# Batch 1 of a sliding-window attention with a gated feed-forward put into the form of batches 2 and 3

## The chip, the cores and the metric

The kernel runs on one core of one Trainium2 chip. The metric is the device time of one execution in microseconds, the median of three runs. A profiled execution gives the trace that the prediction reads.

## The reference

Attention over 4 batches, 8 heads, 768 tokens and heads of 64, in which a query sees the first four tokens (the sinks) and the 128 tokens that end with itself; then a feed-forward without a nonlinearity, whose two gates are multiplied. Inputs and output are float32.

```python
scores = scale * np.matmul(q, k.transpose(0, 1, 3, 2))
keep = (pos[None, :] < 4) | ((rel >= 0) & (rel < 128))       # rel = query - key
a = softmax(np.where(keep, scores, -1e9))
x = np.matmul(a, v).transpose(0, 2, 1, 3).reshape(B * S, H * D)   # 3072 x 512
out = ((x @ w1) * (x @ w2)) @ w3 @ w_out                     # d_ff = 1024
```

## The kernel before

Everything is computed in bfloat16 with float32 sums. `w3 @ w_out` is folded into one matrix `w3o` at the start: the tasks `t3` transpose w3 by row blocks (`fold_w3`), `fm` multiply (`fold_mm`). Its inputs come as raw float32 through SP's queue, with casts on ACT and DVE, or through POOL's queue, which casts in the transfer. Between the first tasks, while the weights arrive, `keep_busy` issues filler matmuls (`pz`).

Then, for each batch:

- POOL issues the loads of k, q (`kqN`) and v (`vN`), a block of 128 tokens each, 128 KB in the chip's memory format. From batch 2 on, a load first waits until the load four before it has landed (`send_load`, the small copies into `spent`).
- k and q are needed with the head's dimension on the partitions (`kqT`). Batches 0 and 1 turn a block with eight TensorE transposes and one DVE copy of PSUM (task `tpk`, line 260 and 262). Batches 2 and 3 turn it with one DMA transpose on SP's queue (task `td`, line 267).
- Scores (`sc`): matmuls of 64 rows, exp on ACT, a mask on DVE. Values (`av`): matmuls, then a reciprocal and a product on DVE that write `xn`. Batches 0 and 1 work by 256 queries, in `scores` and `values` (or by 128 in `block_scores`), and treat the sinks apart: sink scores `ss` (line 312), their exp `es`, sink values `vs`, and one matmul of 130 columns in each `av` beyond the first 256 tokens. Batches 2 and 3, those in `LATE`, work by the units of `CUTS` (320, 224, 224 tokens: `UNITS`, `SPANS`), in `late_scores` and `late_values`. There a block's own keys are copied behind the four sink keys (`own_keys`, task `ko`, tile `kown`), and its values likewise in `vp` and `vN` (`own_values`, task `vo`), so that the sinks need no matmul of their own.
- x is turned: batch 0 with TensorE and a copy on ACT (`xt`), batches 1 to 3 with DMA transposes (`xd`, line 511).
- Gates (`g`, line 524): for each chunk of tokens and each of 8 column blocks, four matmuls with w1, copied by ACT, and four with w2, multiplied on DVE into `ab`. Chunks: 3 x 256 tokens in batches 0 and 1; 320 and 448 in batches 2 and 3.
- Projection (`p`, line 585): eight matmuls of 512 columns for 128 tokens, a copy and an output DMA on SP's queue.

TensorE's order is written out by hand, task by task, in `TURNS`. The order on ACT, DVE and SP follows from a planner in the kernel (`plan`), which runs while the program is built: it has a duration for each stage and an arrival time for each load (`landings`, `service`), picks what could start first, and `LEAN` shifts single choices. Engines run their instructions in that fixed order, so what waits at the head of a queue holds up what stands behind it. PSUM has four buffers for ordinary tasks (`mm`) and two for scores (`sc`). A change between score matmuls and others in TensorE's order is called a turn.

Buffers are shared by tags: `kqN`, `kqT`, `xT`, `ab` and `kown` alternate between two batches, `vp` lies where `wo_sb` was, and `w3T` uses `kown` and `kqN` of batches whose loads come later.

Of the kernel before, what the change touches and what calls it, by code (L numbers as in the profile page):

```python
# [21 lines left out]
def kernel(  # L22
# [13 lines left out]
    nc = tc.nc  # L36
# [17 lines left out]
    LATE = range(2, B)  # L54
# [6 lines left out]
    CHUNKS = [[(256 * i, 256 * i + 256) for i in range(3)]] * 2 + [[SPANS[0], (SPANS[1][0], S)]] * (B - 2)  # L61
    XPOSE = ((2, 0), (2, 1), (2, 2), (3, 0), (3, 1), (3, 2))
# [17 lines left out]
    vc = const.tile([P, 2, D], FP32, name="vc")  # L80
# [23 lines left out]
    vp = [None] * 2 + [inp.tile([P, 4, H, VS], BF16, tag="wo", bufs=1, name=f"vp_{b}") for b in LATE]  # L104
    kown = [None] * 2 + [inp.tile([P, NP, 5, P], BF16, tag=f"kown{b % 2}", bufs=1, name=f"kown_{b}") for b in LATE]
    ksbd = [inp.tile([P, 648], BF16, name=f"ksbd_{b}") for b in range(2)]
    vs = [inp.tile([P, H, D + 1], BF16, name=f"vs_{b}") for b in range(2)]
    es = [inp.tile([P, 512], BF16, name=f"es_{b}") for b in range(2)]
# [15 lines left out]
    def send_load(b, dst, src):  # L124

        if b in LATE and len(sent) >= AHEAD:
            nc.gpsimd.tensor_copy(spent[:], sent[-AHEAD])  # L127
        nc.gpsimd.dma_start(out=dst, in_=src)  # L128
        sent.append(dst[:, 0, 0:1])

    def load_qkv(b, kb):
        for src, dst in ((k, kN), (q, qN)):
            send_load(b, heads(dst[b][:, kb, :]), rows(src, b, kb * P, (kb + 1) * P))
        for s in VSLOTS[kb] if b in LATE else (kb,):
            t0, t1 = KEYS[s] if b in LATE else (kb * P, (kb + 1) * P)
            send_load(b, vN[b][:, s, :, 0:D], rows(v, b, t0, t1))
# [18 lines left out]

    def load(what, *i):
        if what == "qkv":
            if i[1] == 0:
                nc.gpsimd.memset(vN[i[0]][:, :, :, D:VS], 1.0)
            for kb in range(i[1], i[2]):  # L160
                load_qkv(i[0], kb)
# [70 lines left out]
    for b in range(2):  # L232
        nc.gpsimd.tensor_copy(vs[b][:, :, D], ones_s[:])
    for h in range(H):
        r0 = 32 * (h // 2) + 4 * (h % 2)
        nc.sync.dma_start(out=vc[r0:r0 + 4, :, :], in_=v[0:2, h, 0:4, :].rearrange("b s d -> s b d"))
# [17 lines left out]

    def transposes(b, kb):

        tp = ps_mm.tile([P, 2, NP, P], BF16, tag="mm", name="tp")
        for i, src in enumerate((kN[b], qN[b])):
            for r in range(NP):
                nc.tensor.transpose(tp[:, i, r, :], src[:, kb, r * P:(r + 1) * P], ident)  # L260
        yield
        nc.vector.tensor_copy(kqT[b][:, :, :, kb * P:(kb + 1) * P], tp[:])  # L262
# [89 lines left out]
    def late_values(b, r, u):  # L352
# [28 lines left out]
        if r == 0:  # L381
# [50 lines left out]
    def block_values(b, j, r0):  # L432
# [19 lines left out]
        if i == 0 and r0 == 0:  # L452
# [5 lines left out]
    def block_x_transposes(b, j):  # L458
# [6 lines left out]
        nc.scalar.copy(xT[b][:, :, j * P:(j + 1) * P], xt[:])  # L465
        yield

    def values(b, r, t):
# [20 lines left out]
        if r == 0:  # L489
# [5 lines left out]
    def x_transposes(b, r0, t):  # L495

        xt = ps_mm.tile([P, 2, 2, P], BF16, tag="mm", name="xt")
        for r in range(2):
            for i in range(2):
# [4 lines left out]
        nc.scalar.copy(xT[b][:, r0:r0 + 2, t * 256:(t + 1) * 256],  # L504
                       xt[:].rearrange("p r i m -> p r (i m)"))
        yield

    def x_transposes_dma(b, t, i):

        q0, q1 = QB[UNITS[t][i]] if b in LATE else (t * 256 + i * P, t * 256 + i * P + P)  # L510
# [26 lines left out]
    def fold_w3(i, j0, j1):  # L537
# [5 lines left out]
        if i not in w3T:  # L543
            w3T[i] = (flat(kqN[1], "k i s")[:, i * 1024:i * 1024 + 1024].rearrange("p (k n) -> p k n", n=P)
                      if i in (4, 5) else flat(kown[2 + i % 6 // 2], "r m x")[:, i % 2 * 1024:][:, 0:1024].rearrange("p (k n) -> p k n", n=P))
        nc.vector.tensor_copy(w3T[i][:, j0:j1, :], tp[:])  # L546
# [13 lines left out]
    def fold_mm(i, j0, j1):  # L560
# [13 lines left out]
        if j1 == KFF and i >= 4:  # L574
            nc.scalar.copy(w3o[:, i, :], po)
            yield
        elif j1 == KFF and i % 2:
            nc.scalar.copy(w3o[:, i - 1:i + 1, :], held[i // 2][:])
            yield

    def project(b, m, n0, n1):
# [7 lines left out]
        (nc.vector.tensor_copy if n0 == DM // 2 else nc.scalar.copy)(o_sb, po[:])  # L589
# [18 lines left out]
    def service(what, *i):  # L608
        if what == "qkv":
            late = i[0] in LATE  # L610
            return [(0.95 if i[0] == 0 else 0.87 * n, 0.845 * n if 6 * i[0] + kb < 14 else (2.15 if i[0] == 2 else 1.9) * n, [(x, i[0], s)])
                    for kb in range(i[1], i[2])
                    for x, s, n in [("k", kb, 1.0), ("q", kb, 1.0)]
                    + [("v", s, 1.0) for s in (VSLOTS[kb] if late else (kb,))]]
# [6 lines left out]
    def landings(RAW=2.0, POOL=3.0, DGE=1.3, RAMP=(0.75, 1.0)):  # L621
# [6 lines left out]
        while any(at[n] < len(q) for n, q in queues.items()):  # L628
# [11 lines left out]
            for n in busy:  # L640
# [3 lines left out]
                if left[n][at[n]] <= 0.0:  # L644
                    lag, keys = queues[n][at[n]][2:]
                    for key in keys:
                        arrive[key] = now + lag + min(1.5, max(0.0, 0.25 * (now - 36.0))) + min(3.0, max(0.0, 0.1 * (now - 70.0))) + min(4.5, max(0.0, 0.2 * (now - 112.0)))
# [28 lines left out]
    for i in range(KFF):  # L676
        for h in range(2):
# [3 lines left out]
                 [("pe", 0.057 * (j1 - j0)), ("dve", 0.05 + 0.075 * (j1 - j0))],  # L681
                 [x for a, _ in needs for x in a], [x for _, a in needs for x in a],
                 started=[("t3", i, 0)] if i >= SPLIT and h else [folded(i - SPLIT)] if i >= SPLIT else [], ring="mm")
        for h, (j0, j1) in enumerate(FM[i]):
# [4 lines left out]
                 [("pe", 0.216 * (j1 - j0))] + ([("act", 0.6 if i >= 4 else 1.04)] if last and (i % 2 or i >= 4) else []),  # L689
# [6 lines left out]
            if last and (i % 2 or i >= 4):  # L696
                tasks["fm", i, h]["frees"] = ("fm", i if i >= 4 else i - 1, 0)
    unit = []
    last_av = []
    late = []  # L700
    for b in range(B):
        for t in range(NT):
            kbs = (2 * t, 2 * t + 1)
            qk = []
            war = [("av", b - 2, NP - 1, NT - 1)] if b >= 2 else []
            for kb in kbs:
                if (b, t) in XPOSE:
                    qk.append(("td", b, kb))
                    task(qk[-1], 1, transposes_dma(b, kb), [("sp", 2.6), ("dma", 1.2)], war, [("k", b, kb), ("q", b, kb)])
                else:  # L710
                    qk.append(("tpk", b, kb))
                    task(qk[-1], 1, transposes(b, kb), [("pe", 0.45), ("dve", 0.65)],
                         war, [("k", b, kb), ("q", b, kb)], "mm")
            if b in LATE:
                def turned(what, kbs):
                    if (b, 0) in XPOSE:
                        return [("td", b, kb) for kb in kbs]
                    return [("tpk", b, kb) for kb in kbs]
# [9 lines left out]
            else:  # L728
# [3 lines left out]
                elif t == 1:  # L732
                    more = [(n, b, kb) for n in (("td",) if (b, 2) in XPOSE else ("tpk",)) for kb in (4, 5)]
# [320 lines left out]
```

## Time and profile before

| what | us |
|---|---|
| median of three runs | 195.2 (194.99 to 195.25) |
| profiled execution, device time | 194.77 |
| its span in the profile | 193.1 |
| TensorE busy in the span | 186.6 |
| DVE busy | 120.9 |
| ACT busy | 101.9 |
| POOL busy | 88.4 |

The page's parts are: engines' busy time, the span in 40 slices, DMA queues, the chain of work that ended last, and groups of instructions. PE is TensorE, and L followed by a number is a line of the kernel. In a group's row the figures after the bar are busy time, the mean duration of one in nanoseconds, and the idle time of the engine just before them with what ended it. In the chain and in a timeline a row has its start and its length. The granted TensorE clock is full in all slices.

### The profile page before, as it was taken

How to read it: one execution, taken by the hardware profiler on the slowest of the kernel's cores; microseconds unless marked ns; L12 is line 12 of the kernel's file. 1: busy time of each engine (PE TensorE's matmuls, PEld its weight loads, DVE VectorE, ACT ScalarE, POOL GpSimd, SP SyncE). 2: the span in 40 equal slices, each digit the busy share in tenths (PEclk: the TensorE clock that was granted, in tenths of full speed). 3: DMA queues.
4: the chain of work that ended last, by engine and by line, in shares of the span. 5: the costliest groups of instructions: out<-in, count | busy, mean ns of one | idle time of the engine just before them, and what ended most of it. 6: DMA issues, size and time to landing. Idle time of an engine off the chain costs nothing.

```text
span 193.1 us, 4791 instructions
## 1 busy us (share of the span) xinstructions
PE 186.6 (97%) x1879; PEld 123.6 (64%) x1879; DVE 120.9 (63%) x293; ACT 101.9 (53%) x172; POOL 88.4 (46%) x149
## 2 busy tenths in 40 slices
PE   7999989999999999999999999999999999999993
PEld 2454556898768777786987767655555666555442
DVE  4753777846898979668777677474666865223300
ACT  3142279653984867357438664366356562243222
POOL 4399787699997866645764875400000000000000
PEclk9999999999999999999999999999999999999999
DMA  5999999999999999999999999994540033320034
GB/s 222 415 367 171 170 162 197 195 160 154 154 177 170 122 161 132 197 235 141 179 142 142 225 212 143 224 165 137 125 57 0 3 88 94 96 93 0 0 122 149
DMA packets 109718, 29.42 MB, mean 152 GB/s; under 512 B 100352, under 2 KB 105600, under 8 KB 109696
## 3 DMA queue, kind: packets, MB, share of 16 engines
q0 software_dynamic: 81600, 12.59, 97.7%
q1 hardware_dynamic: 27952, 16.47, 36.6%
q8 instruction: 14, 0.23, 0.5%
q10 hardware_dynamic: 144, 0.07, 0.1%
q14 instruction: 8, 0.07, 0.1%
HBM read 29.90 MB, written 6.29 MB: 187 GB/s over the span
## 4 chain that ended last, share of the span: by engine, by line
PE 85%; DMA 8%; POOL 4%; SPq 1%; issue 0%; ACT 0%
PE pg L524 44%; PE po L585 22%; DMA w_sb<-in_moe_w_dram 4%; DMA ab<-in_moe_w_out_dram 3%; PE av L376 3%; PE sc L341 3%; PE av L484 3%; PE tp L260 2%; PE sc L392 2%; POOL kqN L128 2%; PE pw L571 2%; PE av L447 1%; PE sc L414 1%; POOL vN L128 1%; SPq L192 1%; PE xt L463 1%
## 5 line engine op out<-in xcount | busy, mean ns | idle before, releaser
L524 PE MATMUL pg<-xT,w_sb 128*128 128x256 bf16 (+2 forms) x640 | 92.7, 294 | 0.0
L524 PEld LDWEIGHTS <-w_sb 128*128 128x128 bf16 x640 | 59.4, 98 | 22.5 <-issue 0.6
L528 DVE TENSOR_TENSOR ab<-a_sb,pg 128x256 bf16<-128x256 f32 (+2 forms) x80 | 37.4, 472 | 35.9 <-PE pg L524 29.6
L531 ACT COPY a_sb<-pg 128x256 f32<-128x256 f32 (+2 forms) x80 | 33.2, 418 | 36.7 <-PE pg L524 35.7
L585 PE MATMUL po<-w3o,ab 128*128 128x512 bf16 (+2 forms) x208 | 44.4, 363 | 0.0
L585 PEld LDWEIGHTS <-ab 128*128 128x128 bf16 x208 | 19.3, 98 | 18.8 <-issue 0.2
L589 ACT COPY w_sb<-po 128x512 f32<-128x512 f32 (+2 forms) x25 | 14.1, 565 | 24.3 <-PE po L585 24.2
L128 POOL DMA_DIRECT2D vN<-in_v_dram x26 | 23.4, 898 | 3.4 <-issue 1.6
L344 ACT ACTIVATE ex<-sc 128x928 bf16<-128x928 f32 (+1 forms) x24 | 22.6, 973 | 4.3 <-PE sc L341 3.6
L128 POOL DMA_DIRECT2D kqN<-in_k_dram x24 | 21.7, 905 | 2.7 <-issue 1.3
L128 POOL DMA_DIRECT2D kqN<-in_q_dram x24 | 21.7, 906 | 2.5 <-issue 1.3
L397 ACT ACTIVATE ex<-sc 128x1024 bf16<-128x1024 f32 (+1 forms) x16 | 15.2, 973 | 3.8 <-PE sc L392 3.4
L348 DVE TENSOR_TENSOR am<-ex,maskt 128x928 bf16<-128x928 bf16 (+1 forms) x24 | 15.2, 652 | 3.1 <-ACT ex L344 3.1
L383 DVE TENSOR_TENSOR xn<-av,rec 112x256 bf16<-112x256 f32 (+1 forms) x24 | 11.2, 468 | 0.8
L127 POOL CAST spent<-kqN 128x1 f32<-128x1 bf16 x24 | 5.5, 228 | 10.7 <-DMA kqN<-in_q_dram 6.2
L402 DVE TENSOR_TENSOR am<-ex,maskt 128x1024 bf16<-128x1024 bf16 (+1 forms) x16 | 10.1, 650 | 0.1
L376 PEld LDWEIGHTS <-am 128*128 128x128 bf16 x208 | 8.9, 98 | 1.7
L262 DVE COPY kqT<-tp 128x1024 bf16<-128x1024 bf16 x12 | 8.3, 688 | 1.6 <-PE tp L260 1.5
L376 PE MATMUL av<-vN,am 128*128 128x65 bf16 x144 | 9.1, 193 | 0.0
L418 ACT ACTIVATE ex<-sc 128x1024 bf16<-128x1024 f32 x7 | 7.2, 1029 | 3.2 <-PE sc L414 3.2
L571 PE MATMUL ph<-wo_sb,kown 128*128 128x512 bf16 x32 | 8.4, 379 | 0.3 <-DVE kown L546 0.3
L602 PE MATMUL pz<-ksbd 128*128 128x512 bf16 x19 | 6.8, 509 | 1.3 <-DVE ksbd L201 1.3
(83 smaller groups left out, 192.6 us busy)
## 6 DMA issues: line engine op xcount, KB each, us to landing
out_dram<-w_sb SPq DMA_DIRECT2D x20, 256.0 KB
vN<-in_v_dram POOLq DMA_DIRECT2D x26, 128.0 KB, 6.0
kqN<-in_k_dram POOLq DMA_DIRECT2D x24, 128.0 KB, 6.0
kqN<-in_q_dram POOLq DMA_DIRECT2D x24, 128.0 KB, 6.6
w_sb<-in_moe_w_dram POOLq DMA_DIRECT2D x9, 256.0 KB, 8.3
ab<-in_moe_w_dram SPq DMA_DIRECT2D x4, 512.0 KB
ab<-in_moe_w_out_dram SPq DMA_DIRECT2D x2, 512.0 KB
kqN<-in_moe_w_out_dram SPq DMA_DIRECT2D x2, 512.0 KB
```

Of the source, the lines that this page charges most:

```text
L128: nc.gpsimd.dma_start(out=dst, in_=src)
L344: nc.scalar.activation(ex[:, :, 0:n], sc[:, :, 0:n], ACTF.Exp, scale=scale)
L348: nc.vector.tensor_mul(am[:, :, 0:n], ex[:, :, 0:n], maskt[:, mv:mv + 1, 0:n].to_broadcast([P, 2, n]))
L376: nc.tensor.matmul(o, lhs, rhs, start=(x == 0), stop=(x == len(todo) - 1), skip_group_check=True)
L383: nc.vector.tensor_mul(xns[b, u][0:m, 0:n, r, :, :], av[0:m, :, :, 0:D], rec[0:m, 0:n].to_broadcast([m, n, 2, D]))
L397: nc.scalar.activation(ex[:, :, c0:], sc[:, :, c0:], ACTF.Exp, scale=scale)
L524: nc.tensor.matmul(pg[:], w_sb[:, kk, dt * P:(dt + 1) * P], xT[b][:, kk, tk], start=(kk == 0), stop=(kk == NP - 1))
L528: nc.vector.tensor_mul(ab[b][:, dt, tk], gate_a.pop((b, c, dt))[:], pg[:])
L531: nc.scalar.copy(a_sb[:], pg[:])
L571: nc.tensor.matmul(po, w3T[i][:, j, :], wo_sb[:, j, :], start=(j == 0), stop=(j == KFF - 1))
L585: nc.tensor.matmul(po[:], ab[b][:, kk, m * P:(m + 1) * P], w3o[:, kk, n0:n1], start=(kk == 0), stop=(kk == KFF - 1))
L589: (nc.vector.tensor_copy if n0 == DM // 2 else nc.scalar.copy)(o_sb, po[:])
```

## The change

Batch 1 joins `LATE`: its scores, values and copies of own keys and values take the form of batches 2 and 3, and its sink tiles (`vs`, `es`, half of `vc`) and sink tasks go. Its gates are cut in three chunks, 320, 224 and 224 tokens. Of its k and q, blocks 0 to 2 are still turned by TensorE and blocks 3 to 5 now by DMA transposes. Of its x, the first 320 tokens are turned by TensorE (`late_x_transposes`, new) and the rest, as before, by DMA. Its loads are issued with v one block behind k and q, seven of v instead of six, and still without the wait on the fourth load before. `OTHER` names copies that change from ACT to DVE or back. `TURNS` is written anew for the whole kernel, `LEAN` has a shift for nearly every choice, and the planner's arrival times change. `w3T` now uses `kown` of batches 2 and 1. `PAIRED` is empty, so its branches do nothing.

```diff
-    LATE = range(2, B)
+    LATE = range(1, B)
...
-    CHUNKS = [[(256 * i, 256 * i + 256) for i in range(3)]] * 2 + [[SPANS[0], (SPANS[1][0], S)]] * (B - 2)
-    XPOSE = ((2, 0), (2, 1), (2, 2), (3, 0), (3, 1), (3, 2))
+    CHUNKS = [[(256 * i, 256 * i + 256) for i in range(3)], SPANS] + [[SPANS[0], (SPANS[1][0], S)]] * (B - 2)
+    TURNED = ((1, 3), (1, 4), (1, 5)) + tuple((b, kb) for b in (2, 3) for kb in range(NB))
+    PAIRED = ()
...
-    X_XPOSE = ((1, 0), (1, 1), (1, 2), (2, 0), (2, 1), (2, 2), (3, 0), (3, 1), (3, 2))
+    X_TURNED = ((1, 1), (1, 2)) + tuple((b, u) for b in (2, 3) for u in range(NT))
...
+    OTHER = {("fm", 1, 3), ("fm", 7, 3), ("p", 2, 2), ("p", 2, 3), ("p", 2, 5), ("p", 3, 1), ("p", 3, 2), ("p", 3, 4),
+             ("t3", 0, 1), ("t3", 1, 1), ("t3", 2, 1), ("t3", 3, 1), ("t3", 5, 0), ("t3", 6, 1), ("t3", 7, 1), ("tpk",
+             0, 1), ("tpk", 1, 1), ("xt", 0, 0, 0), ("xt", 0, 2, 0), ("xt", 0, 2, 2), ("xt", 1, 0, 0)}
...
-        if b in LATE and len(sent) >= AHEAD:
+        if b >= 2 and len(sent) >= AHEAD:
...
+    def pieces(b, kb0, kb1):
+
+        lag = 1 if b == 1 else 0
+        return [x for n in range(kb0, kb1 + lag)
+                for x in ([("kq", n)] if n < kb1 else []) + ([("v", n - lag)] if n - lag >= kb0 else [])]
...
+    def copier(name, act):
+
+        return nc.scalar.copy if act != (name in OTHER) else nc.vector.tensor_copy
...
+    def late_x_transposes(b, u, i):
+
+        q0, q1 = QB[UNITS[u][i]]
+        m = q1 - q0
+        xt = ps_mm.tile([P, NP, m], BF16, tag="mm", name="xt")
+        for r in range(NP):
+            nc.tensor.transpose(xt[:, r, :], xns[b, u][0:m, i, r, :, :].rearrange("p e d -> p (e d)"), ident[0:m, 0:m])
+        yield
+        copier(("xt", b, u, i), True)(xT[b][:, :, q0:q1], xt[:])
+        yield
...
-                      if i in (4, 5) else flat(kown[2 + i % 6 // 2], "r m x")...
+                      if i in (4, 5) else flat(kown[2 - i % 6 // 2], "r m x")...
...
-            war = [("av", b - 2, NP - 1, NT - 1)] if b >= 2 else []
+            war = [("av", b - 2, NP - 1, NT - 1)] if b >= 2 else [folded(i) for i in range(KFF)] if b in LATE else []
...
-             [("av", b - 1, NP - 1, NT - 1)] if b >= 3 else [],
+             [("av", b - 1, NP - 1, NT - 1)] if b - 1 in LATE else war,
```

The new order of TensorE's tasks (a task is named with its indices: batch, then for scores and values head pair and unit, for gates chunk, column block and half): at the start, row blocks 7 and 6 of w3 take each other's place; ahead of the first transpose of row block 5, `("t3", 5, 1)`, stand two more of the `fm` tasks, one more `sc` and two `av`. Ahead of the first gate that reads the last quarter of w2, `("g", 0, 0, 7, 1)`, stands one gate task less. Around the later batches:

```python
# before, from the scores of batch 3 on, first unit to second
("sc", 3, 0, 0), ("sc", 3, 1, 0), ... ("p", 2, 1), ("p", 2, 0), ... ten gate tasks of ("g", 2, 1, ...), ("sc", 3, 0, 1)
# after: five tasks of chunk ("g", 2, 0, ...) now stand behind ("sc", 3, 0, 0); ahead of ("sc", 3, 0, 1) stand seven
# tasks of ("g", 2, 1, ...) less and ("p", 2, 1) less
# the end, before
("g", 3, 1, 7, 1), ("p", 3, 1), ("p", 3, 4), ("p", 3, 3), ("p", 3, 5, 256), ("p", 3, 2), ("p", 3, 5), ("p", 3, 5, 384)
# the end, after
("g", 3, 1, 6, 1), ("p", 2, 3), ("p", 3, 5, 256), ("p", 3, 2), ("p", 2, 1), ("p", 3, 1), ("p", 3, 4), ("p", 2, 2), ("p", 3, 3),
("p", 3, 0), ("p", 3, 5), ("p", 3, 5, 384)
```

More of the change, by code (lines that the diff above doesn't have):

```diff
@@ L159, in load @@
                 nc.gpsimd.memset(vN[i[0]][:, :, :, D:VS], 1.0)
-            for kb in range(i[1], i[2]):
-                load_qkv(i[0], kb)
+            for what, kb in pieces(*i):
+                (load_v if what == "v" else load_qk)(i[0], kb)
         elif what == "w3":
@@ L231 @@
                             pattern=[[32, NP], [4, 2]], channel_multiplier=-1)
[L232 to L233 removed]
+    nc.gpsimd.tensor_copy(vs[0][:, :, D], ones_s[:])
     for h in range(H):
         r0 = 32 * (h // 2) + 4 * (h % 2)
[L236 removed]
+        nc.sync.dma_start(out=vc[r0:r0 + 4, :, :], in_=v[0:1, h, 0:4, :].rearrange("b s d -> s b d"))
     if hold:
@@ L451, in block_values @@
         nc.vector.reciprocal(rec, av[:, :, :, D:D + 1])
-        if i == 0 and r0 == 0:
+        if (b, t) not in xns:
             xns[b, t] = work.tile([P, 2, NP, 2, D], BF16, tag="xn", bufs=3, name="xn")
@@ L609, in service @@
         if what == "qkv":
[L610 to L614, printed above, removed]
+            return [(0.95 if i[0] == 0 else 0.87, (1.65 if (i[0], s // 2) in PAIRED and x != "v" else 1) * (0.845 if i[0] == 0 else 0.9 if i[0] == 1 else 1.72),
+                     [(x, i[0], n) for n in ((s, s + 1) if (i[0], s // 2) in PAIRED and x != "v" else (s,))])
+                    for y, kb in pieces(*i)
+                    for x, s in ([("k", kb), ("q", kb)] if y == "kq" else
+                                 [("v", s) for s in (VSLOTS[kb] if i[0] in LATE else (kb,))])
+                    if (i[0], kb // 2) not in PAIRED or x == "v" or kb % 2 == 0]
         if what == "w3":
@@ L646, in landings @@
                     for key in keys:
-                        arrive[key] = now + lag + min(1.5, max(0.0, 0.25 * (now - 36.0))) + min(3.0, max(0.0, 0.1 * (now - 70.0))) + min(4.5, max(0.0, 0.2 * (now - 112.0)))
+                        arrive[key] = now + lag + min(1.5, max(0.0, 0.25 * (now - 36.0)))
                     if n == "pool":
```

103 lines of the change are left out of this document (60 added, 43 removed), and 216 rows, old and new, of tables (LEAN, TURNS).

## The prediction

> **What bounds the kernel now.** First the page: the engines' shares, then the chain of waits by engine.
>
> ```profile
> span 193.1 us, 4791 instructions
> ...
> PE 186.6 (97%) x1879; PEld 123.6 (64%) x1879; DVE 120.9 (63%) x293; ACT 101.9 (53%) x172; POOL 88.4 (46%) x149
> ...
> PE 85%; DMA 8%; POOL 4%; SPq 1%; issue 0%; ACT 0%
> ```
>
> TensorE is busy 97% of the span and is 85% of the chain; what is not PE there is the start. Next the waits of PE alone (who, for whom: us in total, times, longest):
>
> ```profile
> PE tp L541 <- DMA w_sb<-in_moe_w_dram: 1.2, 2, 0.7
> PE sc L414 <- DVE kqT L262: 0.3, 1, 0.3
> PE ph L571 <- DVE kown L546: 0.3, 1, 0.3
> ```
>
> Besides the filler's first operand, at the very start, that is the whole list, and all of it lies in the folding of the weights; its last wait stands here, in the timeline of PE (start, length):
>
> ```profile
> 24.77 0.40 PE L541 MATMUL tp<-ident,w_sb 128*128 128x128 bf16 x4 [0.69 <-DMA w_sb<-in_moe_w_dram]
> ```
>
> After 24.77 us PE never waits again. So in this kernel a microsecond of PE work taken out behind 24.77 is a microsecond off the end, unless the new order makes PE wait for data or for a free PSUM buffer; that is the whole question here. DVE and ACT count only through such waits.
>
> **The change, part by part.** Prices of PE work come from the chain of waits (start, length, what, instructions), where neighbours stand end to start:
>
> ```profile
> 56.90 0.44 PE sc L392 x8
> ...
> 59.17 0.45 PE tp L260 x8
> 59.62 0.22 PE xt L500 x4
> ...
> 64.99 0.18 PE av L484 x6
> 65.17 0.44 PE pg L524 x4
> 65.61 0.33 PE sc L392 x6
> 65.94 0.33 PE sp L312 x4
> 66.27 0.33 PE sc L392 x6
> 66.60 0.54 PE pg L524 x4
> ...
> 70.10 0.71 PE av L484 x20
> 70.81 0.55 PE sc L392 x12
> ...
> 85.22 0.55 PE sc L341 x16
> ...
> 92.63 0.30 PE av L376 x10
> ...
> 104.05 0.24 PE av L376 x8
> 104.30 0.51 PE sc L341 x16
> ...
> 121.95 4.89 PE pg L524 x36
> ```
>
> The reader sees a group of matmuls that costs the same wherever it stands, and 0.1 us more where score matmuls begin or end (pg: 0.54 against 0.44).
>
> 1. Keys and queries of blocks 3 to 5: three groups of eight transposes leave PE, 3 x 0.45 = -1.35. They become three DMA transposes on SP's queue; hidden if they land in time (item 7).
> 2. Scores of batch 1. First stretch: two pairs at 0.44 become two at 0.55, +0.22. The rest: 0.55 + 0.33 + 0.33 (sink scores) + 0.33 + 0.55 + 0.55 = 2.64 becomes four pairs' worth at 0.51, and the new order cuts it into five groups instead of four, a turn of 0.1 on either side: 2.24. Sum -0.18.
> 3. Values. First stretch 4 x 0.18 becomes 4 x 0.30, +0.48; the rest 8 x 0.355 becomes 8 x 0.24, -0.92. Sum -0.44. (The sink's matmul goes, sinks come from the first rows of the keys' blocks.)
> 4. x of the first 320 tokens on PE: two blocks of 128 at 0.22 and one of 64, between half and whole of that: +0.55 to +0.66; I take 0.55. Its copies gain a wait for PE (item 7).
> 5. Gates in chunks of 320, 224, 224 instead of 3 x 256. Four matmuls cost 0.437 at 256 columns and 4.89 / 9 = 0.543 at 320, so 1.66 ns per column, and 0.384 at 224: 16 x 0.543 + 32 x 0.384 = 20.98 against 48 x 0.437 = 20.98, nothing. Were 224 no cheaper than 256, it would cost 32 x 0.053 = 1.7. But eight transposes of 128 columns, each with a weight load of its own, take 0.45, 56 ns each, so nothing binds at 109 ns; I take 0.
>
> PE work: -1.35 - 0.18 - 0.44 + 0.55 = -1.4 us. The Trainium skill (TensorE: Matmul & The Clock Gate, Back-to-back issue gap) gives a sustained 81 ns for a load and matmul of 128 columns; by that, items 1 and 4 would be an estimated -1.94 + 0.87, 0.27 us better. The row of 56 ns decides; no stretch here shows 81.
>
> 6. The start. The new order has the same folding work, arranged anew. Ahead of the first transpose of row block 5 of w3 (24.77, its load lands at 24.7) it does two more fold groups (0.43 each), a score unit (0.33) and two value groups (0.23 + 0.12): 1.5 us of work to fill what was idle (1.2 + 0.3 + 0.3 in the waits) or filler. But the last quarter of w2 caps the gain:
>
> ```profile
> 30.58 0.75 POOL L140 DMA_DIRECT2D w_sb<-in_moe_w_dram  x1
> DMA to landing us min/median/max: 10.0/10.0/10.0
> ```
>
> It lands at 40.6. Its first gate ran at 41.75 (third group of four in the row below), and the new order has the same work ahead of it but for one gate group less and one score group more, 0.24 less: it would come at 41.5 without a gain, so the gain is at most 0.9. Downwards it can vanish, or cost some tenths where seven evictions of w3's transposes move to ACT. I take -0.6.
>
> ```profile
> 40.88 2.35 PE L524 MATMUL pg<-xT,w_sb 128*128 128x256 bf16 x20
> ```
>
> 7. New waits. DVE: batch 1 now copies its own keys and values as the later batches do.
>
> ```profile
> L262 DVE COPY kqT<-tp 128x1024 bf16<-128x1024 bf16 x12 | 8.3, 688 | 1.6 <-PE tp L260 1.5
> L290 DVE COPY vN<-vN 4x1152 bf16<-4x1152 bf16 (+1 forms) x6 | 2.7, 447 | 0.3
> L287 DVE COPY vp<-vN 128x576 bf16<-128x576 bf16 (+1 forms) x6 | 2.1, 351 | 0.0
> L281 DVE COPY kown<-kqT 128x496 bf16<-128x496 bf16 x8 | 1.9, 288 | 0.0
> 50.00:82.00 32.00, 32.00 (x416) 23.88 (x414) 27.45 (x70) 22.12 (x35) 24.19 (x39) 1.00 2.01 159
> ```
>
> These served two batches, so one batch adds half of 2.7 + 2.1 + 1.9, 3.4, and with two smaller copies some 4; three kqT evictions (2.1), the sinks' products and one eviction given to ACT (1.7 by the same sizes) go: about +0.5 to +2 on a DVE that was busy 27.45 of 32 us (third figure of the last row, a window of 50 to 82 us) while PE never waited. Bound: 0 to 1 us. The x copies of batch 1 lie about 1 us ahead of the first gate that reads them, with one of the three on that DVE: 0 to 0.5.
>
> Data: here is the queue of loads (POOL) and of transposes (SP).
>
> ```profile
> 41.22 0.89 POOL L128 DMA_DIRECT2D kqN<-in_k_dram  x1
> 55.96 1.02 POOL L128 DMA_DIRECT2D vN<-in_v_dram  x1
> 59.02 0.88 POOL L128 DMA_DIRECT2D kqN<-in_k_dram  x1 [0.30 <-issue]
> 121.85 0.88 POOL L128 DMA_DIRECT2D vN<-in_v_dram  x1
> 74.94 1.24 SPq L267 DMA_TRANSPOSE kqT<-kqN  x1
> 82.84 0.28 DVE L278 COPY kown<-kqT 128x496 bf16<-128x496 bf16 x1
> ```
>
> Batch 1's 18 loads go out every 14.74 / 17 = 0.87 us, the 38 of batches 2, 3 every 62.83 / 37 = 1.70. The excess, some 31 us, goes with what SP sends in that stretch: 9 transposes of k, q (256 KB), 13 of x (112 to 128 KB) and 9 outputs (256 KB), 6.2 MB, so about 5 us per MB: 1.3 per k, q transpose, 0.6 per x. The change adds three of the first and takes two of the second off (and four get smaller), +2.5, and one more load, +0.9: loads of batch 3 land some 3.4 us later (L). A transpose reaches its reader within 7.9 us (74.94 to 82.84). What this does to PE is the first rival; for the likely case I take 0.4 us of waits from all of item 7.
>
> **Sum:** -1.4 - 0.6 + 0.4 = -1.6 us. The profiled execution took 194.77 us (span 193.1 and 1.67 around it), 0.43 below the median of 195.2; so 193.2 against itself and 193.6 on the median. 0.2% (0.39 us) is what a measurement can tell from no change.
>
> **Rivals.**
>
> A, slower: batch 3 arrives late. The new order moves its scores up (seven gate groups and a projection go behind them) while its loads move back.
>
> ```profile
> 115.36 0.88 POOL L128 DMA_DIRECT2D kqN<-in_q_dram  x1 [0.27 <-issue]
> DMA to landing us min/median/max: 5.3/5.3/5.3
> 142.67 0.51 PE sc L341 x16
> ```
>
> q of its block 4 lands at 115.36 + 5.3 = 120.7 now; with 7.9 for the transpose and 0.6 for the copies of its keys that makes 129.2 + L. The scores that need it start at 142.67, and in the new order at that less seven gate groups (4 x 189 ns, by item 5's slope, is 0.756 each at 448 columns), less a projection (eight matmuls at 512 columns by the same slope, 1.73) and less the 2.0 of items 1 to 6: 133.6. So PE starts to wait at L = 4.4 and all that is gained is gone at L = 6.4. At L = 6.9 to 7.4 the time is 195.7 to 196.2. Against it: L is 3.4 by the rows and 7.9 is an upper bound. Chance 0.13. The Trainium skill (VectorE: DVE Perf Modes, The three transpose paths) speaks against this change too: it puts a 128x128 transpose at 390 ns on TensorE and 1309 ns by DMA and advises TensorE where PSUM will do; by it 24 such tiles take an estimated 31 us of DMA and give TensorE back 9. The trace agrees that the DMA way is the longer one (up to 7.9 us for eight tiles against 0.45), and has PE, not the DMA, as the bound.
>
> B, nothing: DVE's queue is the bound in batch 1 (90% and more between 50 and 90 us), PSUM buffers come free late, and PE loses the 1.4 to 2 that it was spared: 194.9 to 195.4. For it: 27.45 of 32. Against: the share was that high without a single PE wait. Chance 0.12.
>
> C, less: the start gives nothing or loses a little, the rest holds: 194.2 to 194.6. Chance 0.2.
>
> D, as summed, 192.7 to 194.1, likeliest 193.6. Chance 0.55.
>
> **Numbers.** 193.6; range 192.7 to 195.4 (D, C, B and the near part of A; 192.7 is the sum with the start at -0.9 and no waits). Faster: D, C and a little of B, 0.77; same 0.11; slower 0.12.
>
> **What would show it.** Right: kqT evictions 12 to 9, DMA transposes of kqT 12 to 15 and of xT 20 to 18, loads of v 26 to 27, PE busy near 184.5, no PE wait behind the folding, t3 of row block 5 still near 24.8 and the first gate near 33.5 (34.5 before). Wrong, by A: PE waits before sc L341 or pg of batches 2, 3 for a DVE kown copy or a DMA, SP waiting longer on kqN loads. By B: PE waits for DVE releases between 50 and 90 us. By C: as much idle and filler before 40 us as now.

## The result, and the profile after

| | before | after |
|---|---|---|
| median, all executions (20 each) | 195.34 us (194.86 to 196.82) | 195.24 us (192.94 to 199.02) |
| ratio to before, of the executions kept | | 0.9923, 95% interval 0.9894 to 0.9952 |
| profiled execution | 194.77 | 193.17 |
| its span | 193.1 | 191.5 |

The change takes 0.8%, 1.5 us, off the executions that the ratio keeps, and nothing off the median of all twenty. The ratio leaves out eight of the changed kernel's executions (196.0 to 199.0) for their length alone: five of them had the full clock, three a mean granted clock of 0.991. The twelve that are left still spread over 2.4 us, from 192.9 to 195.35. Most experiments below ask why.

The page after, engines and chain:

```profile
span 191.5 us, 4799 instructions
...
PE 184.6 (96%) x1874; PEld 122.3 (64%) x1893; DVE 125.9 (66%) x302; ACT 102.5 (54%) x171; POOL 91.5 (48%) x149
...
DMA  6999999999999999999999999999511022000525
...
PE 76%; DMA 13%; POOL 6%; issue 1%; SPq 1%; ACT 0%
```

PE is still the bound. Its last matmul ends 1.51 us earlier (188.23 against 189.74). Its busy time is 2.0 us less, but part of that is only records that the trace lacks: it has 1874 matmuls for 1893 weight loads, where before there were 1879 of each. The DMA engines are 90% busy or more from 5 to 134 us (27 slices of 4.8 us); before, they were from 5 to 130. The DMA in the chain is the front: the first gate that reads the last quarter of w2 waits for it. PE's waits (who, for whom: us in total, times, longest), and that row in PE's timeline:

```profile
PE pz L649 <- DVE ksbd L226: 1.3, 1, 1.3
PE ph L618 <- DVE wo_sb L598: 0.3, 1, 0.3
PE ph L618 <- DVE kown L593: 0.3, 1, 0.3
PE tp L588 <- DVE w_sb L598: 0.2, 1, 0.2
PE pw L618 <- issue: 0.2, 1, 0.2
PE pg L571 <- DMA w_sb<-in_moe_w_dram: 0.2, 1, 0.2
```

```profile
25.38 0.61 PE L588 MATMUL tp<-ident,w_sb 128*128 128x128 bf16 x8
33.23 1.04 PE L571 MATMUL pg<-xT,w_sb 128*128 128x256 bf16 x8
40.87 3.67 PE L571 MATMUL pg<-xT,w_sb 128*128 128x256 bf16 x32 [0.16 <-DMA w_sb<-in_moe_w_dram]
```

Row block 5 of w3 is reached at 25.38 and no longer waits; the first gate comes at 33.23 (34.47 before). After 40.87 PE waits for nothing. The prices of the new work, in the chain (start, length, what, instructions):

```profile
62.27 0.71 PE av L412 x20
69.25 0.77 PE xt L550 x12
95.43 1.92 PE pg L571 x20
134.13 0.51 PE sc L377 x16
```

Two pairs' values cost 0.61 and a turn, x of 320 tokens 0.77, and four gate matmuls of 224 columns 0.384 (1.92 / 5). But DVE's timeline shows how near data comes to being late:

```profile
133.10 0.29 DVE L317 COPY kown<-kqT 128x496 bf16<-128x496 bf16 x1 [0.44 <-DMA kqT<-kqN]
134.50 0.49 DVE L317 COPY kown<-kqT 128x496 bf16<-128x496 bf16 x2 [1.11 <-DMA kqT<-kqN]
```

The first row copies batch 3's keys of block 4, which have just come out of their transpose; the scores that read the copies start 0.67 later, at 134.06. The second copies the keys of the last stretch, not needed before 141.84, and while it waits 1.11 us a normalisation, a gate product and a mask product stand behind it.

### The profile page after: what moved, and what is told of

The parts are those of the page before. It is cut to its first block, busy times and chain, and to the rows that moved or that the text cites. A ratio compares the mean times of both kernels' runs of the same rounds, so it can differ in the third digit from the quotient of the medians.

```text
span 191.5 us, 4799 instructions
## 1 busy us (share of the span) xinstructions
PE 184.6 (96%) x1874; PEld 122.3 (64%) x1893; DVE 125.9 (66%) x302; ACT 102.5 (54%) x171; POOL 91.5 (48%) x149
## 4 chain that ended last, share of the span: by engine, by line
PE 76%; DMA 13%; POOL 6%; issue 1%; SPq 1%; ACT 0%
PE pg L571 42%; PE po L632 21%; DMA w_sb<-in_moe_w_dram 5%; PE av L412 5%; PE sc L377 5%; DMA vN<-in_v_dram 4%; DMA ab<-in_moe_w_out_dram 4%; POOL w_sb L159 3%; POOL kqN L132 2%; PE tp L295 1%; SPq L217 1%; PE av L520 1%; PE sc L428 1%; POOL vN L132 0%; ACT w_sb L636 0%
## 5 line engine op out<-in xcount | busy, mean ns | idle before, releaser
L571 PE MATMUL pg<-xT,w_sb 128*128 128x256 bf16 (+3 forms) x640 | 91.5, 294 | 0.2 <-DMA w_sb<-in_moe_w_dram 0.2
L578 ACT COPY a_sb<-pg 128x256 f32<-128x256 f32 (+3 forms) x80 | 32.6, 417 | 34.1 <-PE pg L571 31.9
L575 DVE TENSOR_TENSOR ab<-a_sb,pg 128x256 bf16<-128x256 f32 (+3 forms) x80 | 37.1, 471 | 19.4 <-PE pg L571 18.1
L380 ACT ACTIVATE ex<-sc 128x928 bf16<-128x928 f32 (+1 forms) x36 | 34.4, 972 | 5.0 <-PE sc L377 4.7
L384 DVE TENSOR_TENSOR am<-ex,maskt 128x928 bf16<-128x928 bf16 (+1 forms) x36 | 23.1, 651 | 1.2 <-ACT ex L380 1.1
L419 DVE TENSOR_TENSOR xn<-av,rec 112x256 bf16<-112x256 f32 (+1 forms) x36 | 16.9, 469 | 1.2
L416 DVE RECIPROCAL rec<-av 112x4 f32<-112x4 f32 (+1 forms) x36 | 6.6, 183 | 10.9 <-PE av L412 10.6
L636 DVE COPY w_sb<-po 128x512 f32<-128x512 f32 (+1 forms) x7 | 4.3, 633 | 10.5 <-PE po L632 7.3
L377 PE MATMUL sc<-kqT 64*128 64x112 bf16 (+3 forms) x168 | 10.0, 218 | 0.0
L377 PEld LDWEIGHTS <-kqT 64*128 64x128 bf16 x168 | 6.8, 94 | 3.5 <-issue 3.0
L377 PE MATMUL sc<-kqT,kown 64*128 64x112 bf16 (+2 forms) x120 | 8.7, 208 | 0.0
```

What stands on the lines that cost most here:

```text
L377: nc.tensor.matmul(sc[:, e, c:c + m], keys[hp], qT[b][hp, r, q0:q0 + m], start=True, stop=True)
L380: nc.scalar.activation(ex[:, :, 0:n], sc[:, :, 0:n], ACTF.Exp, scale=scale)
L384: nc.vector.tensor_mul(am[:, :, 0:n], ex[:, :, 0:n], maskt[:, mv:mv + 1, 0:n].to_broadcast([P, 2, n]))
L419: nc.vector.tensor_mul(xns[b, u][0:m, 0:n, r, :, :], av[0:m, :, :, 0:D], rec[0:m, 0:n].to_broadcast([m, n, 2, D]))
L571: nc.tensor.matmul(pg[:], w_sb[:, kk, dt * P:(dt + 1) * P], xT[b][:, kk, tk], start=(kk == 0), stop=(kk == NP - 1))
L575: nc.vector.tensor_mul(ab[b][:, dt, tk], gate_a.pop((b, c, dt))[:], pg[:])
```

## The experiments

The theory: PE's work makes the time, and the spread comes from late data. The change sends more through DMA engines that were full, so batch 3's keys land with 0.7 us of room, and what is late waits at the head of DVE's queue. The rivals: the spread comes from the start; DVE's own load is the bound. One execution of kq_te (493.18 us, the profiled one) and one of ahead3 (663.54) are far out, for a cause that no run shows.

| run | executions | median, all | lowest | ratio to before, of those kept |
|---|---|---|---|---|
| again | 6 | 193.9 | 192.62 | 0.9879 (0.9839 to 0.9918) |
| tail | 6 | 199.2 | 197.85 | 1.0153 (1.0119 to 1.0187) |
| kq_te | 6 | 206.77 | 204.42 | 1.0533 (1.0488 to 1.0579) |
| kq_te_held | 12 | 194.47 | 193.95 | 0.9955 (0.9933 to 0.9976) |
| old_front | 6 | 205.51 | 203.66 | 1.0491 (1.0440 to 1.0542) |
| front_held | 12 | 195.25 | 193.69 | 0.9955 (0.9927 to 0.9984) |
| ahead6 | 6 | 202.52 | 201.41 | 1.0360 (1.0325 to 1.0396) |
| ahead3 | 4 | 204.76 | 203.19 | 1.0454 (1.0396 to 1.0512) |
| light | 6 | 193.26 | 192.98 | 0.9877 (0.9848 to 0.9905) |
| heavy | 6 | 201.75 | 199.75 | 1.0292 (1.0249 to 1.0335) |
| ko_late | 6 | 193.59 | 192.57 | 0.9881 (0.9834 to 0.9929) |
| ko_sc_late | 6 | 193.03 | 192.62 | 0.9880 (0.9841 to 0.9920) |

**again.** No edit.

> The changed kernel once more, nothing altered. In its first profile PE waits for no data after 40.87 us, but two transfers land close ahead of their readers: k, q of block 4 of batch 1 at 68.5, its copies end at 69.4 and the scores start at 70.46 (1.0 us of room), and k, q of block 4 of batch 3 at 133.1, copies to 133.4, scores at 134.06 (0.7 us). Single times lie between 192.9 and 199. Theory (late data): those two rooms run out in the longer executions; where this profile is over 194, PE waits in front of the second stretch of scores of batch 1 or 3 (sc L377) by the excess, and DVE's kown copies wait for the transposes. Rival (start): the excess lies ahead of 45 us, in the folding or at the last quarter of w2. Both: a profile of 193.0 to 193.4 if nothing is late.

Four executions at the full clock (192.62, 192.67, 193.11, 194.69) confirm the result; a fifth took 196.49. The profiled execution (316.28) was granted 0.564 of the clock and says nothing on the question.

**old_front and front_held: what the start is worth.** Both give the first 85 tasks of `TURNS` their old order, shifts and eviction engines. In the second a list also holds ACT, DVE and SP behind the start to the order that they have in the changed kernel.

```diff
-    TURNS = [("t3", 0, 0), ("t3", 0, 1), ...          # first 85 as after
+    TURNS = [("t3", 0, 0), ("t3", 0, 1), ...          # first 85 as before
# front_held alone, in plan():
+                         if when(q) is not None and in_turn(e, q[3])]
```

> The changed kernel with its first 85 tasks on TensorE (the folding and the first gates, to 40.9 us; the same set in both kernels) in the order and with the queue biases of the kernel before, and their evictions on the engines that they had before. Theory: it gives back what stood between the two profiles behind these tasks, 41.31 against 40.87, 0.44: a profile of 193.6 (193.4 to 193.9), and the first gate that reads the last quarter of w2 waits no more. Rival: the start gave nothing, since something behind it waits for data anyway, 193.1 to 193.3. Rival (spread comes from the start): single times within 1.5 us.

> The changed kernel with its first 85 tasks on TensorE in the order, biases and eviction engines of the kernel before, as in the run old_front; but behind them ACT, DVE and SP now keep, instruction for instruction, the order that they have in the changed kernel, where old_front had let the planner order them anew. Theory (the 10 us of old_front came from DVE's new order in batch 1, with am queued behind copies of keys and values; the start itself is worth 0.44): a profile of 193.4 to 193.9 and single times as of the changed kernel. Rival (the start itself is worth more, since all that follows depends on when it ends): 196 and more again, with PE waiting for DVE am between 55 and 70 us.

old_front missed by 10 us. Its PE and DVE timelines, 56 to 60 us:

```profile
59.31 0.29 PE L519 MATMUL av<-vN,am 128*128 128x65 bf16 x4 [2.73 <-DVE am L437]
```

```profile
56.63 0.42 DVE L574 TENSOR_TENSOR ab<-a_sb,pg 128x256 bf16<-128x256 f32 x1 [0.76 <-PE pg L570]
56.97 0.30 DVE L322 COPY vp<-vN 128x576 bf16<-128x576 bf16 x1
57.19 0.68 DVE L296 COPY kqT<-tp 128x1024 bf16<-128x1024 bf16 x1
57.98 0.47 DVE L313 COPY kown<-kqT 128x496 bf16<-128x496 bf16 x1
58.37 0.28 DVE L325 COPY vN<-vN 4x576 bf16<-4x576 bf16 x1
58.58 0.67 DVE L437 TENSOR_TENSOR am<-ex,maskt 128x1024 bf16<-128x1024 bf16 x1
```

PE stands 2.73 us for a mask product with five other items ahead of it on DVE: the planner, fed with other times at the start, had ordered DVE's queue anew, batch 1 included. With that order held, lowest time and ratio come back to 193.69 and 0.9955: the other order of ACT, DVE and SP was 10 us. In front_held's profile the first 85 tasks end 0.57 later than after's (41.45 against 40.87), near the expected 0.44. Its time, 196.76 at full clock where 193.4 to 193.9 was expected, has one wait behind the start. PE, then DVE:

```profile
139.39 2.43 PE L570 MATMUL pg<-xT,w_sb 128*128 128x448 bf16 x12 [2.60 <-DVE xn L418]
```

```profile
134.00 0.29 DVE L316 COPY kown<-kqT 128x496 bf16<-128x496 bf16 x1 [0.59 <-DMA kqT<-kqN]
138.15 0.49 DVE L316 COPY kown<-kqT 128x496 bf16<-128x496 bf16 x2 [3.86 <-DMA kqT<-kqN]
```

It is the place shown above for the changed kernel, with 3.86 us in place of 1.11; the normalisation behind it is what PE waits for. The run also settles a rival: with the start of the kernel before, its twelve executions still spread from 193.69 to 201.18, so the new start is not what spreads the times.

**kq_te and kq_te_held: item 1 undone.** Three `tpk` tasks are put into `TURNS`; the second run holds the other queues.

```diff
-    TURNED = ((1, 3), (1, 4), (1, 5)) + tuple(...)
+    TURNED = () + tuple(...)
```

> The changed kernel with k, q of batch 1's blocks 3 to 5 turned by TensorE again, three groups of eight transposes put in after the first scores of batch 1, ahead of the next projection and ahead of the x of batch 1. Theory: PE has 1.35 us more work and no wait behind the folding, so a profile of 194.5 (194.3 to 194.8); the loads of batch 3 land 2 to 4 us earlier (q of block 4 at 121.5 to 123.5 instead of 125.45), so both rooms grow and the single times lie within 1.5 us of the lowest. Rival (DVE is what holds the stretch from 50 to 80 us): three more evictions of 0.69 us make PE wait there and the profile is 195 or more. Rival (start): spread as in the changed kernel.

> The changed kernel with k, q of batch 1's blocks 3 to 5 turned by TensorE again at the same places as in the run kq_te, but ACT, DVE and SP keep the order of the changed kernel; only the three evictions are put in between. Theory: three groups at 0.45 on PE and nothing else, +1.35: a profile of 194.4 to 194.8, loads of batch 3 that land 2 to 4 us earlier (q of its block 4 before 123.5 instead of at 125.45), and single times within 1.5 us of the lowest. Rival (DVE holds the stretch from 50 to 80 us, so that the change's gain was DVE's): PE waits there for evictions, and 195.5 or more. Rival (late data is not what spreads the times): spread up to 198 as now.

kq_te took 206.8 where kq_te_held took 194.5: again 12 us from the order of the other queues alone. In kq_te_held PE waits only at its very start, and the profile (194.03) is 0.86 over after's. The three groups cost 1.63 (0.54 each, with turns beside some), and x came out 0.2 dearer; the start, which the edit does not touch, came out 0.55 better, so single profiles differ by half a microsecond there; another 0.4 came back in small pieces behind it. The rival with DVE as the bound falls: three more evictions there, and no PE wait. q of batch 3's block 4 landed at 122.75, 2.7 earlier. Eleven of twelve executions lie between 193.95 and 195.47: dearer than the changed kernel at its best and steadier, with a median over all of 194.47 where the changed kernel's 20 have 195.24.

**tail: more room by the old order of the last 111 tasks.**

> The changed kernel with its last 111 tasks on TensorE (from 111.7 us on, the same set in both kernels) in the order and with the queue biases of the kernel before; nothing ahead of that is altered. The scores of batch 3's second stretch move from 134.1 to about 140.8, 7 us of room instead of 0.7. By the groups of the two profiles these 111 tasks took 76.49 us after and 76.16 before, so the profile comes to 192.7 to 193.0. Theory (late data in batch 3): single times keep within 1.5 us of the lowest, as those of the kernel before do, and the median falls below 193.8. Rival (late data in batch 1, or the start): the spread up to 198 stays and the median stays near 195.

It missed by 5 to 6 us. Its order and shifts came from a planner that had other arrival times, and DVE copies values of batch 3 too early. DVE, then PE, in the profiled execution (201.35; the lowest took 197.85):

```profile
125.66 0.46 DVE L323 COPY vp<-vN 128x1152 bf16<-128x1152 bf16 x1 [3.03 <-DMA vN<-in_v_dram]
```

```profile
127.12 4.34 PE L571 MATMUL pg<-xT,w_sb 128*128 128x320 bf16 x20 [3.62 <-DVE ab L575]
```

So tail doesn't answer its question; it shows the mechanism at another place.

**ahead6 and ahead3: loads held back less, and more.**

```diff
-    AHEAD = 4
+    AHEAD = 6      # ahead3: 3
```

> The changed kernel, but a load of batch 2 or 3 waits for the load six ahead of it instead of four ahead; order on PE, ACT, DVE and SP is the same. Theory (late data spreads the times): POOL's waits of 16 us for landings shrink and the loads of batch 3 land some 3 us earlier, unless the transposes on SP's queue slow down by as much (5 to 8 us each now); if they do land earlier, single times stay within 1.5 us of the lowest and the median is 193 to 193.5. Rival (the transposes get their share only because the loads are held back): transposes take 9 us and more, as the first two of batch 1 do now (9.1 and 9.7 while loads go out unheld), the scores of batch 2 and 3 wait for them, and the time is 196 or more. Rival (nothing waits for data): no change in median or spread.

> The changed kernel, but a load of batch 2 or 3 waits for the load three ahead of it instead of four ahead; order on PE, ACT, DVE and SP is the same. Three loads in 5.3 to 6 us of flight are 1.9 a load instead of 1.72: the last lands some 7 us later. Theory (rooms of 0.7 and 1.0 us, so lateness goes almost in full to the end): PE waits in front of the scores of batch 2 and 3, DVE waits for kqT with am and gate products queued behind, and the time is 197 to 200. Rival (room is larger than these rows say, since DVE's and PE's queues absorb it): below 195.

Both lose, by 8.5 and 10.3 us (201.41 and 203.19 against 192.94, lowest against lowest). Six in flight bring the loads no sooner (the last lands at 138.5, after's at 132.3); each takes longer, and so do the transposes of k and q: from 71 us on, but for the last one, 6.6 to 11.5 us, where the changed kernel has 5.1 to 8.0. k's loads on the page of after, then of ahead6 (median us to landing), and PE's waits in ahead6:

```profile
kqN<-in_k_dram POOLq DMA_DIRECT2D x24, 128.0 KB, 6.1
```

```profile
kqN<-in_k_dram POOLq DMA_DIRECT2D x24, 128.0 KB, 8.5
```

```profile
PE pg L571 <- issue: 2.9, 1, 2.9
PE pg L571 <- DMA xT<-xn: 2.1, 1, 2.1
...
PE sc L377 <- DMA kqT<-kqN: 1.1, 1, 1.1
```

The rival written for ahead6 holds: the transposes get their share because the loads are held back. Three in flight land the last load at 142.2, and three of its four times, 203 to 206, lie even above the 197 to 200 that was expected: the rival, that the queues absorb the lateness, falls.

**light and heavy: less and more DMA, all else the same.** light leaves out the output transfers of batch 0, heavy sends them twice.

```diff
-        for c in range(n0, n1, step):
+        for c in range(n0, n1 if b else n0, step):                    # light
...
+            if b == 0:                                                # heavy
+                nc.sync.dma_start(out=out[t0 + 3 * S:t0 + 3 * S + P, c:c + step], in_=o_sb[:, c - n0:c - n0 + step])
```

> The changed kernel without the six transfers that write the output rows of batch 0 (1.5 MB of the 6.2 MB that SP sends between 48 and 132 us; these rows are not written). Order on PE, ACT, DVE and POOL is the same. Theory (the DMA engines, 90% busy and more to 134 us, are what makes data late): loads of batch 3 land 4 to 7 us earlier (q of its block 4 at 118 to 121.5 instead of 125.45), no wait of DVE for kqT is left, times 192.6 to 193.4 with nearly all within 1 us of the lowest, and no gain beyond that, since PE is the bound of the rest. Rival (spread from the start or the clock): times up to 197 as now.

> The opposite of light: the changed kernel sends the output rows of batch 0 twice, the second time to the rows of batch 3, which are written over later with their own (1.5 MB more on SP's queue between 48 and 87 us). Order on PE, ACT, DVE and POOL is the same. Without these transfers q of batch 3's block 4 landed 3.1 us earlier and the transposes of batch 1 some 2.8 us earlier; with them twice I expect as much later. Theory (rooms of 1.0 and 0.7 us; what is late waits in DVE's queue): PE waits 1 to 2 us in front of the second stretch of scores of batch 1 (70 to 72 us), DVE waits 3 us and more for kqT between 132 and 142 us with PE losing 2 to 4 us there, and all runs lie at 196 to 200, where the changed kernel's longer runs lie. Rival (lateness is absorbed by the queues, and the spread is something else that light happened to hide): 193 to 197 as the changed kernel.

light: all six executions lie between 192.98 and 193.78, none lower than the changed kernel's best, where 12 of the changed kernel's 20 lie more than 1.5 us above its lowest. q of block 4 landed at 122.39, 3.1 earlier (4 to 7 expected); a wait of 0.48 us for kqT was left on DVE. heavy: all over 199.7 (196 to 200 expected), with q of block 4 at 132.25, 6.8 later (3.1 expected). Its DVE and PE timelines:

```profile
63.44 0.46 DVE L323 COPY vp<-vN 128x1152 bf16<-128x1152 bf16 x1 [2.94 <-DMA vN<-in_v_dram]
...
140.31 0.29 DVE L317 COPY kown<-kqT 128x496 bf16<-128x496 bf16 x1 [3.33 <-DMA kqT<-kqN]
```

```profile
64.56 0.48 PE L412 MATMUL av<-vN,am 128*128 128x65 bf16 x10 [1.87 <-DVE am L384]
138.74 2.44 PE L571 MATMUL pg<-xT,w_sb 128*128 128x448 bf16 x12 [2.77 <-DMA xT<-xn]
```

Between the two lie 3 MB on the DMA queues, 1.5 less and 1.5 more than in the changed kernel, and they decide between 193.3 and 201.8, with PE's order the same. I had named the places only in part: batch 1 was held by its values, not by its keys, and late in the kernel PE waited for x of batch 2 ahead of the keys of batch 3. The unaltered kernel is not known to have run on light's chip, so how much of light's small spread is the chip's isn't shown; heavy's loss of over 5 us, with its waits in the trace, doesn't hang on that.

**ko_late and ko_sc_late: the blocked place cleared.** The copies for batch 3's last stretch go behind the normalisation of `("av", 3, 0, 1)` in DVE's order. ko_sc_late also moves `("sc", 3, 0, 1)` and `("sc", 3, 1, 1)` two gates back.

```diff
 # DVE's order
-("ko", 3, 1), ("ko", 3, 2), ("av", 3, 2, 0), ..., ("av", 3, 0, 1)
+("av", 3, 2, 0), ("ko", 3, 1), ..., ("av", 3, 0, 1), ("ko", 3, 2)
```

> The changed kernel with two items of DVE's queue moved and nothing else: the copies of the keys of batch 3's last stretch (first read by TensorE at 141.84) go from right behind those of the stretch before to behind the normalisation of its first values (138.4), and one normalisation goes ahead of both. In the profile of front_held these copies waited 3.86 us for their transpose, with a normalisation, a gate product and the products with the mask queued behind them, and PE lost 2.60; in the changed kernel's own profile they waited 1.11 and PE lost nothing. Theory (late data of batch 3, blocked in DVE's queue, is what spreads the times): lowest times as now, 192.6 to 193.2, median 193 to 194.2, and at most a fifth of the runs over 1.5 us above the lowest, where the changed kernel had some 40%. Rival (the spread has another place): as now, median 193.9 to 195.2. A profile over 194 shows the other place.

> As ko_late, and the first two groups of scores of batch 3's second stretch go two gate groups (1.5 us) back on TensorE, with the gate copy on ACT and the gate product on DVE that belong to these gates ahead of them: 2.2 us of room instead of 0.7 for the keys of block 4. Theory: if that transpose is the second thing that comes late, the runs draw together further, median 192.9 to 193.6. Rival (the copies moved in ko_late were all of it, or neither is): no difference from ko_late.

In both profiles the waits of DVE for kqT are gone, and PE's waits behind 45 us come to 0.4 us in the one and to none in the other. ko_sc_late has the lowest median of all (193.03, six executions from 192.62 to 194.71) and beats the kernel before by 1.2%, but its interval overlaps the changed kernel's, so that it beats this one too isn't shown: the run again, unaltered, has the same ratio (0.9879). ko_late still had a 194.76 and a 195.73. front_held shows that the place can cost 2.6 us; that it spreads the changed kernel's own times isn't shown. No readable profile caught the unaltered kernel in a long execution; where it loses there stays open, and that late data does it is inferred from light, heavy and front_held. A hint lies in the clock: three of its eight long executions (197.08, 197.87, 199.02) have a mean granted clock of 0.991, which is what one stretch of 3.41 us at half the clock makes of it (an estimate, 1 - 0.5 x 3.41 / 195), and in the traces of ahead6, ahead3, old_front and tail such a stretch comes with a wait of PE of 2.7 us or more (last section). In these three PE probably stood still once for about that long; what it waited for they don't tell.

## Why the prediction was right, point by point

The forecast, 193.2 against the profiled execution's own 194.77, met 193.17; the ratio puts the kernel at 193.8 where 193.6 was forecast, and the median of all twenty, 195.24, lies at the upper end of the range. Part of the agreement is luck: the items below missed by up to 0.28 us, and in both directions, so that the sum is off by only 0.1. The ratio's interval is 0.3% to either side, wider than the 0.2% that the prediction took for the least that can be told. Measured prices are from PE's timelines: from each task's first matmul to that of the next, summed over the tasks of a kind.

| step | predicted | measured |
|---|---|---|
| 1 k, q off PE | -1.35 | -1.35 (six groups 2.79, three 1.44) |
| 2 scores, sink scores | -0.18 | -0.34 |
| 3 values | -0.44 | -0.38 |
| 4 x on PE | +0.55 to 0.66 | +0.75 |
| 5 gates of batch 1 | 0 | +0.13 (21.39 to 21.52) |
| 6 start, after the same 85 tasks | -0.6 | -0.44 (41.31 to 40.87) |
| 7 waits, and all else on PE | +0.4 | +0.12 |
| end of PE | -1.6 | -1.51 (189.74 to 188.23) |

Items 1 and 5 came out by their rows; four matmuls of 224 columns cost 0.384 to the digit, so the upper end of +1.7 was empty. Item 2 misread the kernel before: of the first stretch's pairs, the first two stand apart in TensorE's order, 0.27 each, so the stretch cost 0.98 and not 0.88. Item 4 was mis-sized: the block of 64 tokens takes 0.22, as much as one of 128. Its four transposes start some 30 ns apart where the others start 56 apart, but the first of the next block starts only 0.12 after the last of them; and another 0.1 lies behind the last block. Item 6 was right in its cap: the start was 0.76 ahead (40.12 against 40.88) when it met the last quarter of w2, which took 0.32 back; row block 5 stopped waiting since more work stands ahead of it. In item 7 the forecast of 0.5 to 2 us more work for DVE between 50 and 82 us was wrong in sign:

```profile
50.00:82.00 32.00, 31.84 (x416) 24.30 (x417) 26.09 (x69) 22.68 (x38) 22.58 (x36) 1.00 2.06 161
82.00:140.00 58.00, 57.57 (x669) 40.65 (x674) 45.21 (x119) 35.45 (x62) 30.84 (x53) 1.00 1.74 182
```

DVE has 26.09 us there (27.45 before). Its extra work came later, 45.21 against 39.11 in the second window, since the new order moves batch 3 forward. Rival B has nothing to stand on, and its "90% and more between 50 and 90 us" was a misreading: 27.45 of 32 are 86%, and of the slices of 4.8 us from 48 to 92 in the page of before only three of nine show a 9:

```profile
DVE  4753777846898979668777677474666865223300
```

The step that failed is the size of L, the lateness of batch 3's loads. q of batch 3's block 4 landed at 125.45, 4.8 later and not 3.4. POOL's timeline:

```profile
62.53 0.88 POOL L132 DMA_DIRECT2D kqN<-in_k_dram  x1 [0.30 <-issue]
...
126.17 0.89 POOL L132 DMA_DIRECT2D vN<-in_v_dram  x1
```

The rate of the later loads was as predicted (63.64 / 37 = 1.72). But the first of them started at 62.53, 3.5 behind before's 59.02. The first two new transposes meet loads that nothing holds back, took 9.1 and 9.7 us (issued 55.39 and 58.74, semaphores set at 64.5 and 68.5), and the last two loads of batch 1 took 10.5 and 11.6 us beside them, where the last of before took 5.7. That is not all of it, as kq_te_held shows, which has none of the three transposes:

```profile
61.08 0.88 POOL L132 DMA_DIRECT2D kqN<-in_k_dram  x1
```

Its first held load is still 2.1 behind before's, and its q of block 4, at 122.75, still 2.1 late. So some 2.7 of the 4.8 go with the three transposes, which the sum had at 3.9 (3 x 1.3), and some 2.1 with the rest, which the sum had at -0.5 (+0.9 for the extra load, -1.4 for x). The rest is the term that was mis-sized; what it holds besides the extra load stays open, and single profiles differ by half a microsecond here.

By rival A's own condition PE waits from L = 4.4; it didn't, since the transpose at the critical place took 6.3 us (126.75 to 133.1) and not the 7.9 of the bound. That bound was one transpose's and not the longest: in the same trace of before, one issued at 69.70 set its semaphore 8.1 later. The room was 0.7 us. So A was not refuted but just missed: it is what happened in heavy and in front_held's profile, and that the changed kernel's long executions meet it is inferred. If they do, its chance of 0.13 was too low for the median over all executions.

The Trainium skill (VectorE: DVE Perf Modes, Rules for kernel authors) advises TensorE for such tiles where the result may go to PSUM. Here both sides have a price: the DMA way frees 1.35 us of PE, and puts some 2.7 us of lateness on the loads. kq_te_held, which follows the advice in batch 1, is 0.9 dearer in the profile and 1.0 in the lowest time (193.95 against 192.94); its median over all executions is 0.8 lower.

## What to carry to other kernels

When work moves from the engine that is the bound to DMA engines that are already 90% busy, the gain can show in the best execution and the price in the spread, as here: look for the copies that wait for a transfer with other work queued behind them, and count how many tenths of a microsecond the transfer has to spare. A copy that is needed late should stand late in its engine's queue. And an experiment that moves one engine's work must hold the order of the others, or it measures the planner: here 10 and 12 us of it.

## What the runs showed of the hardware that was not expected

The time of a DMA transpose goes with the loads around it: in the changed kernel, 9.1 and 9.7 us for the first two, while loads go out unheld, 5.0 to 8.0 with four in flight, 2.3 to 3.3 once they have ended. The runs with other numbers in flight confirm it: the transposes of k and q from 71 us on, but for the last one, with which the loads end, took 3.1 to 5.3 us with three in flight, 5.1 to 8.0 with four, 6.6 to 11.5 with six. Three and six both cost the kernel over 8 us; its orders were laid out for four, and others weren't laid out for three or six.

A stall of PE can cost more than itself. In tail the 20 gate matmuls behind the wait of 3.62 us took 4.34, where 20 at 0.136 (0.543 / 4) take 2.7. The window of just these, in tail (busy time and instructions of PE, PEld, DVE, ACT, POOL, then PE's granted clock):

```profile
127.12:131.46 4.34, 4.34 (x22) 2.53 (x23) 1.66 (x4) 0.85 (x2) 2.09 (x5) 0.65 2.30 181
```

The clock was at 0.65, and full again from 131.5 on. Length alone doesn't decide: behind a wait of 2.92 in ahead6 twelve matmuls of 448 columns took 4.11, behind one of 3.30 in ahead3 the usual 2.43. Behind the wait of 2.73 in old_front, too, the clock fell to half, 0.4 us after PE had started again at 59.31, and stayed there for 3.41 us; in ahead3 it did the same behind a wait of 2.83, 1.3 us after PE had started again. Waits of 2.60 (front_held) and 2.77 (heavy) left it full. PE in ahead6, in ahead3, and the window in old_front:

```profile
138.52 4.11 PE L571 MATMUL pg<-xT,w_sb 128*128 128x448 bf16 x12 [2.92 <-issue]
```

```profile
146.06 2.43 PE L571 MATMUL pg<-xT,w_sb 128*128 128x448 bf16 x12 [3.30 <-DVE xn L419]
```

```profile
59.69:63.10 3.41, 3.41 (x25) 2.41 (x21) 1.73 (x5) 1.33 (x3) 1.18 (x3) 0.50 1.90 128
```

The Trainium skill (TensorE: Matmul & The Clock Gate, Part 1: The HAM clock gate) lets the clock fall after an idle window of about 3.4 us and rise after as long a busy one, with a window that runs freely. The length of the slow stretch agrees with these rows, and a free phase would fit that a longer wait left the clock full where shorter ones did not. That waits of 2.73 to 2.92 us were enough does not agree, and the measurement decides.
